# A second order table for a kernel whose instruction order is written out: fillers and transfers placed anew

## The chip, the cores and the metric

The kernel runs on one core of a Trainium2 chip. Five engines work side by side, each through its own instructions in the order in which they were issued: TensorE (PE in the profile, its weight loads PEld), VectorE (DVE), ScalarE (ACT), GpSimd (POOL) and SyncE (SP). SP does no arithmetic here: it issues every transfer between the device's memory and the on-chip buffers. The metric is the device time of one launch in microseconds (us), the median of three runs.

## The reference

The input `x` and the logits `f_logit` are 4 batches of 6272 time steps with 256 channels. First a gated recurrence runs along time, then a block that multiplies two projections with a third one that was convolved (circularly, over all 6272 steps) with a long filter:

```
f = lower_bound + (1 - lower_bound) * sigmoid(f_logit);   i = 1 - f
h[t] = f[t] * h[t-1] + i[t] * x[t]            # for every batch and channel
x1, x2, x3 = split(h @ w_proj, 3)             # 256 -> 3 x 256
conv = irfft(rfft(x2, time) * rfft(filter, time), time)
out = (x1 * conv * x3) @ w_out                # 256 -> 256
```

## The kernel before

The time axis of 6272 steps is taken as 128 x 49, so the transform is done in two steps of matrix products: one over the 128 (D1), one over the 49 with its twiddle factors (FT), and back (VA and VB, then ID). Four batches follow one another, and the work on the recurrence of batch b+1 is laid over the end of batch b.

The program is not written in the order in which it runs. `Plan.op` records operations: a kind, the engines that may do it, what it reads and writes, its function. `Plan.emit` then issues them in the order that a long string, `ORDER`, holds: three characters per operation give its number, its engine and its bank of PSUM (`Plan.order`). `emit` asserts that all that an operation depends on was issued before it. Each engine then runs its own operations in that order and waits by semaphores for the others. So the string decides three things: each engine's sequence (SP's too, hence the order of the transfers), who does a copy that two engines may do, and the PSUM banks. There are 2325 operations.

In what follows an operation is named by its kind and its number among its kind: `ff3` is the fourth load of filter rows. The kinds, with the lines of the kernel before:

- `warm` (L561): 32 fillers of TensorE, four products of a constant each, whose results nobody reads.
- `ff` (L579, SP): 13 loads of filter rows, 512 KB each (the last 128 KB), into ten buffers, so `ff10` to `ff12` wait for a buffer. `fr` (a copy, L270, L275 or L280): to one of two staging buffers. `rot` (L590, PE): a rotation of the rows, `f2` (two copies each, ACT or DVE): its result out of PSUM.
- `FF1`, `afs`, `FF2`, `hw`, `hst` (L615, copies, L633, L272 or L277, L641): the transform of the filter in 16 units; `FF1` needs all `f2`. `hst` (two per unit, 196 KB and 128 KB) stores the spectrum into the device's memory. `last` (L650) is the zero frequency's part.
- `args`, `tabs`, `rest`, `pad` (DVE, POOL): tables of sines and zeroed edges, made once.
- `load` (L308, SP): 13 chunks of 512 time steps per batch, two loads a chunk, an even number for `f_logit` (tile FL) and an odd one for `x` (tile XT), 512 KB each, the last chunk's 128 KB; three buffers, so the loads of chunk c wait for the transposes of chunk c-3. Chunk c of batch b has `load` 26b+2c and 26b+2c+1.
- `sig` (L311, ACT), `u` (L313, POOL), `su` (L325, PE), `f` (L338 ACT or L340 DVE), `scan` (L346, DVE): sigmoid, product with x, transposes to channels on the partitions, gate, recurrence. `su`, `f` and `scan` come twice per chunk. `wrap` copies the first 3072 steps of a batch behind its end.
- `P` (L673) and `x2`: the projection of x2, 13 groups, which need all scans of the batch. `F1` (L686), `A`, `F2` (L745), `prod` (L758, DVE), `I2` (L768), `Th`: 16 units of forward step, product with the spectrum, first inverse step. `H` (L723, SP) loads a unit's spectrum, 392 KB, into one of three buffers (tile Hu), which in the front are the staging of `hw` and `hst`.
- `x13` (L373), `xs`, `z` (L389, POOL): the other two projections and their product.
- `I1` (L802), `y` (L808, DVE), `proj` (L820), `o`, `store` (L830, SP): second inverse step, gate, output projection, and 13 stores of 512 KB a batch out of three buffers; they need all `Th` of the batch.

The numbers behind `ORDER` come from a planner that is not part of the kernel; the `cost`, `dma` and `lag` values that stand in the calls of `op` are not used at run time and are the same in both kernels.

Of the kernel before, what the change touches and what calls it, by code (L numbers as in the profile page):

```python
# [58 lines left out]
class Plan:  # L59
# [55 lines left out]


ORDER = (
    "A8gAAYBBgAOYABIAjQBLgACIBGgAtRBQgBVgAhSBagBkgAdTA7YAPIAxUBfgA9AA2VBpgAwWBCAA0XBugBDQA+SBFABMYBzgAyUBEAARIAvV"
    "BHYBACAqWA/CBNUA1XAQAB4gAmQERgBIRBWYAkWAcTBRAADgAYYAuXAnQBJBAgWBKBESgBSWAzTBUGBbYBXQBTGEpgAeSBYIBgYASABcSBPE"
    "BlIEdgAaYBZABhWBqABOMBmQEegBeKBdCBvYBrUBjOBnAEqgAUIBoAB0YAGgBwSBiOA4QATIBxCB5YB1WByKAFgAlRBsMB2GB6SAiQB7CBtM"  # L120
    "B8CA5RETAB3OAfQAWICISCBUCJKCKQEUYB/WCLACRSCCECAOA3QEfACNUAEYCOMCDYEVWErAEZQEgYEWGCEUE1gEaAE2gEXOCFEEbIEsYEhW"
    "ElUEiGCTQFBgCSCEjOFCgANACaSCQgAVYEmECMYCUIEtWCbCEnMAIACVYCWQAXYE3AExSEuOApUFNgAHAEyKArVE4YFOgCXACcUCHgEzKCGg"
    "AJAA6QFDAClQEvOE5SALACdEFEYCmIE9WE6CCjUE+OFZgAKAFagAsQE7KCkECYgCsQAMACeYFFUFPAEcYE/OCfSFGEFQYCgCFJWFHMFjgFKG"
    "CoSFkgCtACuUFLOCPgEwYCpCFRQE0YCvMFbAFVWCnYFSIC3SFtgFcYFWOFugAoUC4CCigC1UFTICZgCxSC2EFXOC6UCyCFAYFdQCwYFlAFMY"
    "FgSC7MC+WC5YF3gE8AFmYFhKF4gDAUC/GChgFeIDBECqgDJWCzgFfIAbUFvADCYFnUDKGFiKDDQFwYFoEFqWDEAFpMDHSGBgCrgDQQDICC0g"
    "FrODSUGCgFIYDRADbSFsOF5ADLYDMQDTMFxWDcCF6YDNIDVUFyGF0SDWEFzODZQGLgF1CC8gDiUFUYC9gDaADkWF2KGMgDUYDjEDdYDtQDGg"
    "B9YGDADFgDeUDlOF7SDuADfMDnWF8CDmYF+QDoGF9KD2UGEYGVgF/ADXgDrWDOgD3ED0SDsOD/UGWgD1CGAIDwWB+YDPgFYAGNADvYGFSD4Y"
    "EAMEoYD9QDxGGGKDggD5UGOYDhgGHKD+AGIWDYgD6EEGQMVgGJOEISDzgEHAGKOEBYGPUGXAEYAGSQEJCGQMECWGTAMhgEKYGYYGRMEPSDqg"
    "EDGDpgAZYEQCGUIGZWELUGaGEkYGcSJSQGbOGdCMtgEMEGeKJTRDygGfgEEgGmWJVJJUAENgMXAD8gJWYG4SGnOGgUEFgEOgG2QG5KD7gG0W"
    "G3AGhMGsSMjAGyQGtKG1GGqUMvAGiWGrMGkSGjGHLgGoUGlKHEgMigGwWGpEMWgHSgGuSGxGJXUGvKGzAJYVJcWJaFJdXJZMG8QJfHJeOJbY"  # L130
    "G6SG9AG+UG7KJhXJgYG/EHAQJiWHBAHFSJkOJmUJjHHHKJnVJoEJlYHCQHMWJpFHIKJrUJqYJsSJtEHDIJwVHZgJuCHiTHOOHGYJxQJvYHjD"
    "J1RJyNJ2SJzAHJTHPOJ3BJ0YHgVJ4CHTQHKDHqgHNYJ6XHUYHVIHhFJ5YHkSJ7UHlCHWIHQVJ/QJ9EHbYHRNHaSHxgJ8HKARKBAJ+YHcKHmU"
    "KCBHrWHnEMkYHdKHXQKESHYAHtOH4gHeUKGCIGQHuOKDYHfEHoSKFWIHAHyUHpKH/gKJXKHGH0MMugHsYIIQKLHKIYHvSIJAH1MH5WHzYHwC"
    "H6YIKQMYYH7OIQgKKUILAH2SH8OIAVH3CIMQICNKMEIXgH9SINAKNYKOXIDNKPUH+CKTVIBYKQHIOQIegIRSIPIKVFIsWKREITKIEQItGKSY"
    "KUVIUKKYUKWFKZSISYKaEKXYIYWIlgIFAKdVIaOKbCKeTIZYIVQKfFKcYIbOKgDIfUIWAKiSIhMI2gIuWIcQIvGIiMImTInYKkCKhYI3WIpL"
    "IdAI9gKjVKnSIgYKlFIwQIoLKpCKmYIjUIxAKoSJEgI5OKsTMwYKqCIqQIkEI6OKtSIrAMZUKvKKuDI+WJLgKrYMaEMdQJAOIySMeAM5gKwY"
    "M6gIzCMbMKxWKzGMlSMfIKyUMmCK2VJBOK0EK3WK4FMpQK1YK5GMnKI0UNFgMqAMxWK6YNGgI1MM7AM1SMrIK7UMgYNRgMyGK8VI4YNSgI/Y"
    "K9EM8YMzOI7QM2CLAUK+FM3KJFWI8ALBVLCEK/YJHOM9QLDFNBSNHALEYJIOLFUNdgM+ALGVNegLHENIYM/IJCWNCCLKUNTANDKJMQJDGJGY"
    "JOINJSNUYLIFNNWNKCJPINngNOGNogNfANLKLJYNVQLMELLVNPOLPUNWANgYNZSLRELNFNXILQUNxgNaCJJWNygLSERSVNbKLOYJKGNhQNpA"
    "NkWJNYNiILTYRTUN7gNlGRUNJQSN8gNqYRVENjIRXVJRCRYUNmORZFLZQRaELUSNzAMsYLaINrUNuWNsEN0YLVKOFgLbQNvGOGgNtMLWSLcA"  # L140
    "McYNwON9ALeULjQLXCN+YLfMN1WM0AN4SLYgLkIN2GLdgLoUOPgN5CN3OOQgLgQOHANAAN6KOIYLlWLhALpMLtSLigLmGN/QLuKNQYOCUOAA"
    "LqWOagMoAOBIOZgODELngLySLrGOEMOJQORAOMWLsgLzKLvUUVgONGOSYOKAOOOL0SLwEOLIL3WM4YObAOTULxgNMAL4ONEYOWQOUENYYUhg"
    "L1COcYOVML8WUigOXAOdSL2gL9OL5UOeCNcAOfKL+WL6EOYIOgSUXAMBUOhKMGQOiKL/GOrSMHIMAgOvWOsCMCMUugOnQUWgOwGUtgO5SL7g"
    "OoAOzUO6KOlWO0EOjQOmOOxSOkAOpUUjAO1WOqMOyCMDQO2GO7SMEIOtUO8CMLWOuEMQQO3SMMOUvAMIUO4CUwYMNWMRIMJMO9QMOGO/SO+I"
    "PBUPACRWYPDWPCMPHQPEGRbYPNSPJIPFWRcURdVReEPGORhQRfFPKIPgWRjARgYRiUPhGRmVPQKPZgPiQPIYRkEPLWPjAPPKPTTPUYRlYRoF"
    "PaQPVLPqgPMGRnSRrVPOYRpCPWLPRWRtFPmSPSGPbYPcIRqYPkUPxgPnCPXWPdIRsQPlEPrSPYGRwRP4gPtKPoURuAPeWRyBPpMRvYRxQPuK"
    "PyRRzAPsYQGUPfGPzYUYYP1JP/gR1QQHEPvWP0JP5SR3AQIUPwGP7KR0YQQgP2QQJEQAWP8KP6YP3AQKUQBYR2SQLEQCOP9QQXgR4CR6TQDO"
    "QRUP+AR5YR7WR8DQTMQMQQegR9GUkYR/SMPgQNAQEWQUMQYTSBCQFGQOQSASQaLQlgR+YSEVMKgSCCSFWQPIUZSSDYSGFQbLQuQSHGSJXQvA"
    "QSYUaKQsVSIYQ2gSKUSLPQtFQVQUbKQZYSOXSMEQfVQWASNYSPUQhNSQHQwSSREQcQQxCQiNQmUQnYSSYQdAQySQpMQ9gUdWQzCQgYSTQQoM"
    "UeGSURQjSSVAUfOREgSWBQqUU5gQkCSXYU6gQ0QQ3WQ1IUgAMFgQ+SQrEQ5OQ/YSYQSZRSaASdURAKSbBSeVSfEUlQScYQ6OSgFSiWUmASjS"  # L150
    "Q4YSkGRBKShYRLgSnUSlCSoVU7AQ7WUnISmYRFSSqFSpMQ8GU8YUpQRHKSsVUqAVFgStUVGgSuFRCWRIKSvESxSSrYRDGSyVUrIRMTSwYUxW"
    "S0FRPLU1QSzCUyGS2VRGYVRgS1YROLS3SVSgS4FS7US5CS8VRNYUzOVHARJSS6YU2AS+NRQWVIYRKCU3ITAVRRGU9SS9ETBQU+KTCFVBWS/Y"
    "TDIVTAVJUVdgU/KTFRVegTEYVCGTGQTHBVDOVNSTIAVUYTKRVKEVngTLQTMBVogVLMMSWVOCTNATPRVPKTJYVVUTQQVWEMTOTOYVZSTRJTSA"
    "TUWVfAVXMVygTTYZSQMUgZTRVaCVxgVQYTVOZXUZUAVgYZYVZVBZZMZaFTWWVpAVbKTZQTXGU4YVhUTaIVqYVkSViETYgTeWV7gVlCVjMTbQ"
    "V8gUcAVmKTcAVrUVsETfOTjQTdgVzAVuSTkITgWWFgVMAV0YVvCVtMTlQU0AThGVwKToUV9ATigV1WWGgTpMV4SV2GV+YWPgV5CV3OTqUWQg"
    "TmAV6KTtWTngTrEUsYTyQVcYTuOWHAV/STsgWCUVAATzITvWWagWDEWZgWACWEMT3QWIYTwGWBKT8UUoATxgT0WWRAT4IVEYWJSWSYT9MWMQ"
    "WKCWNAWLKT5UT1GVYYWOIUBST2gT6EWTWUCKWWQWUGT7gT+UWbAcVgWVOWXAWcYUDST/EWYIWdWUAgWgUWeGchgWhEULQWfOUECctgWiMUGW"
    "cWgW3UUHOcugcigWvSUFgW4EUMIW5WWwKWzUW6GWlQW0EWjSWmAWtWWkKcXAW7UWrQcjAW8MWpSWsAWxUcYYWuGW1QWyMcvAWnWW2AUIUWoO"
    "WqCckYUNQUJMW9SUOAUQWW+KXBUW/QUROXAAXDSXCMZWYXHWXECXNQXKOZcUZbYXFSZdVZeEXGKZhXZfFXJOXgSZjHZgYXiUXhCZiXXQIXZg"
    "ZmWXIYZkHcZSXOYZoGXPIZlYcaCcdWXjEZnRcbKc6gZrQXqgceGZsUc5gZtIclSZpBcfOZuEXRQZqYcmCXaUXSAcnKXbYXmWXLQXnGXcMcpS"  # L160
    "XUYXMAZvYXTWXdMdFgZwUcqCZxQZyEXWOZ1RZzAXkUZ3BZ0YZ2QXVOXlEZ6XZ7RcwYcrKZ8HXeUXxgZ4AX4gXXWXfEdGgZ9JXoSc7AXYOXyU"
    "Z5YYIQXpKXrWYJAYGSc8YXtOcxQYHCXuOZ/WcyAaASaBGZ+YaETX1MX/gaCCaFXdHAXzYX0Mc1VXsYaDYaGDaJSdSgaHHczIXvTdRgc2FaIY"
    "YQgaKXXwDc3NX2QdIYaLCX5TX3AaOSX8LaMHaPVaQCYKQaRFX7LYAWaNYYLAYMUYDOaTSYXgYBYYNEaUTaSYaYQYCOaVCaZRaWDX6Yc9UaaA"
    "aXYYOSYegadXc+EYPKUKgaeWabBc/MYESdTAX9QagOafHYRUYSYX+AacYaiWYUMYFCYsQYZYajXYtAahYYTMYYSanVakGYaKc0YYlgYVQalH"
    "apFYuWamYYbKYWAYfUaoSYvGcgYYiMY2gYwQYgYaqCdUYYcWYxAYhMYmSasVYdGYoKY9gYyQauFYnYYjWarYYzAYpKY3UYkGY0QatSY1IZEg"
    "ccAaxTY5MYqWazDavCdBQY6MYrGawYY+TaySdCAZALa2WZLga0CY/Ya3XY4Yddga4Ga1Ya7VUPgdDIa5HY7SdegZMWcsYa9FZBLZFQa6YY8C"
    "a8VZHIZCSa+FbAUa/YZDCZPObBVbFQbCEdJSZGYbDFZIIbHAdNUbEYdKCbGXZOOdogZJQdngZNYbIHc4YdLKUSWZKAbJYdfAbKQdOMbLRdVS"
    "UTGdPMdgYbMAdZWbNBbPQdWCdxgdaObQRbRAdygZQUdXKbSBUUgbOYhSQZREhTRdbOdhSbTYhVBbZUhUAdMYdkWdpAbaMbUQd7gdlGdqYd8g"
    "bVIhXUdiChYVdzAdjKbWQhZEdAYdmOhaFbeSd0YbXAdrUbfKduWdsEbYgbbQeFgdvGdtMeGgd1SbcAdwObjUd9Ad4QbdgbkMbgWePgd2Cd+Y"
    "eQgd5Ad3KblUbhGd6IboSbmEbigdEYd/WeHAcoYbpKbngbtUeCQeIYbuMbqSeDAeZgeageAGeEIbvUbrCeBObyQbsgeRAeJSbzIeMWeKCeSY"  # L170
    "eNGeLKb0QeOObwEb8SdYYdQAeTUbxgb9Kb3Wb1Ab4OeWSeUEb2gcBQeXCeVMb5WebAecYeYKb+Ub6GcCIb/EcGSb7gedWeeOegUcDQefOehE"
    "dcAeiMcHKexWezUeyGcISe0McEAerWcJKe7QesGelUcKgepSe8AcAgetWeqKemEe5QeuGe3Ue6AcQScLWe4EcRKevQcMOe1SewIhWYenUe2C"
    "hbYejWeoMhcQekGhdRheIhhShfBe9ThjKhiVhgYe+De/WfBQfAOhkFfDSfCAhlYfHUhmWfECfKMhnXfNQhpHfJMfFShrVhoGhsXhqYhtFfGK"
    "hwWfZghuHfgUfQIhxShvYhyGh1TfhEfPIfiWfIYh2RhzCfLUfjOfqgh4Bh0Yh6Qh3DfTRfMEfOYh7TfWJh5Yh8AfRWh9DfkUfVJfSGh+YfaS"
    "flEh/QfcKfxgfUYfmWfbYiARfnGiBIiEUiFVfdKiCBfXWiGEiDYfrQfYGf4gfoSiJUfpKiHFgGWftIiIYiKVgHGfeSiLMiMFiOQfsYfzYfuI"
    "gIWffCiNYfyUiQAf5Sf1MgJGf/giPRiTQiRBf0MfvWiVAiSYiUVfwGf8Kf2QgQgf6YiWFgKWf3Af7KiXYgAUgLGgMQgDMgBYgXgf9SgNAiYW"
    "gCMiZXiaGgRQf+CgOVidUgeggPNibHcFggsSgTIgSYgEVicYgtCieXifMgFFiiQgUIguSigHgYUikAihYgfWglggbMgvCijRinQgZYilBgaM"
    "gVSipAgwQgWCggYghOimYg2ggcUgxAgmSgiOgnYgdEioWgyQiqGgpKg9ggjUgzAirYisXgkMitWiuHixTivGgoKg0Qg3UizDiwYg+Wg1IiyT"
    "hEgg6Mi2Sg4Yi0DgqQi4Ci1Yi3Tg5MgrAi7Vi8Si9FhBOhLgg7Qi5DjAUi+Ci6YhAOjBVg8AhFSg/YhMQjCEhHKi/YhCWjDFjFUhIKjEYhDG"
    "jGVjKSjHEcNWhOIhGYjIFjJYjLThPIhJUjNDjMCjPQhNYhKEjQTjOYjRIhQRjSLcSUhRBjTYcOGjUQjZScTEjVIcPgjeWcUgjjUjaKjWQjbS"  # L180
    "jXAjfOjcCjYgjkMjgQjdgjoWjhAjtSjpOjlUjigjqQjmEjuKjyWjngj3UjrAjzOjvSjsgj0QjwCj4Mj8Wjxgj5Sj9Oj1AkBUj2gkGQj6CkCM"
    "j+Wj7gkDSj/GkHIkLUkAgkIWkECkMMkFgkQQkNSkJOkRIkKgkSUkOCkPgkTEkUg"
)


# [706 lines left out]
```

## Time and profile before

| | |
|---|---|
| median of three runs | 476.97 us (475.66, 476.97, 477.04) |
| profiled execution, first to last instruction (its span) | 476.4 us |
| HBM read, written | 80.93 MB, 31.00 MB; 235 GB/s over the span |
| granted TensorE clock, mean | 0.998 |

The profile is of one execution, and its span is its own time; the median of the three runs is 0.6 us longer. `A <- B` in a group names what is written and what is read; "idle before" is the time in which an engine waited, with what ended the wait. The milestones of the profiled execution, read from the timeline:

| batch | first scan | last scan ends | first P | last P ends | first I1 | last store issued |
|---|---|---|---|---|---|---|
| 0 | 29.6 | 78.8 | 78.7 | 89.7 | 153.6 | 253.5 |
| 1 | 130.7 | 178.3 | 178.3 | 191.0 | 252.5 | 355.4 |
| 2 | 222.3 | 282.5 | 282.7 | 293.6 | 357.0 | 451.4 |
| 3 | 303.8 | 386.5 | 386.6 | 399.3 | 449.6 | 472.7 |

The stretch up to 78.7 us, in which the filter is transformed and batch 0's recurrence runs, is called the front.

### The profile page before, as it was taken

What the parts mean: (1) busy time and instruction counts of PE and PEld (TensorE: products, weight loads), DVE (VectorE), ACT (ScalarE), POOL (GpSimd) and SP (SyncE); (2) the same over time, 40 slices, a digit from 0 to 9 for tenths busy, and PEclk for the clock granted to TensorE, in tenths of its full rate; (3) what the DMA queues carried; (4) which work ended last, traced back from release to release, by engine and by line L of the source; (5) the groups of instructions that cost most, each with busy time, mean ns of one, the idle gap of its engine ahead of it and who ended that gap; (6) DMA issues with size and microseconds to landing.
All of it is one profiled execution on the core that took longest, in us unless ns stands there. A gap on an engine that the chain in (4) does not pass through costs nothing.

```text
span 476.4 us, 14713 instructions
## 1 busy us (share of the span) xinstructions
PE 447.8 (94%) x6041; PEld 345.4 (72%) x6041; DVE 424.9 (89%) x457; ACT 416.1 (87%) x606; POOL 297.9 (63%) x309
## 2 busy tenths in 40 slices
PE   8888999999998999999999999999999799999995
PEld 7776777866756879776666889666767697676784
DVE  8778989799999996999999996999999877999874
ACT  5899898899999998889999978999999778999763
POOL 6777784287889730668798734688787504766600
PEclk9999999999999999999999999999999999999999
DMA  8989998636588897157769995567588831356277
GB/s 329 396 310 317 313 342 251 227 104 216 165 289 306 289 328 279 41 164 226 244 230 312 345 338 219 145 205 235 163 271 270 341 135 46 110 152 193 77 279 277
DMA packets 39841, 112.88 MB, mean 237 GB/s; under 512 B 4258, under 2 KB 6178, under 8 KB 39774
## 3 DMA queue, kind: packets, MB, share of 16 engines
q1 hardware_dynamic: 39774, 111.94, 69.0%
q8 instruction: 47, 0.77, 0.6%
q14 instruction: 20, 0.16, 0.1%
HBM read 80.93 MB, written 31.00 MB: 235 GB/s over the span
## 4 chain that ended last, share of the span: by engine, by line
PE 52%; DVE 16%; DMA 12%; POOL 6%; ACT 6%; issue 6%; SPq 0%; ACTq 0%; DVEq 0%; POOLq 0%
PE PS L373 13%; PE PS L673 9%; DVE HA L346 8%; PE PS L768 8%; PE PS L745 6%; PE PS L686 5%; DVE ys L808 5%; PE PS L325 4%; DMA XT<-in_x_dram 4%; DMA X<-in_moe_filter_fft_dram 4%; PE PS L820 3%; POOL zt L389 3%; POOL XT L313 3%; DMA out_dram<-osb 2%; DVE PP L758 2%
## 5 line engine op out<-in xcount | busy, mean ns | idle before, releaser
L389 POOL TENSOR_TENSOR zt<-x1s,x3s 128x490 f16<-128x490 f32 (+1 forms) x104 | 125.5, 1214 | 67.1 <-ACT x3s L270 33.0
L313 POOL TENSOR_TENSOR XT<-XT,FL 128x1024 f32<-128x1024 f32 (+1 forms) x52 | 116.9, 2248 | 64.7 <-ACT FL L311 41.8
L758 DVE TENSOR_TENSOR PP<-PS,Hu 98x1008 f16<-98x1008 f32 x128 | 146.5, 1198 | 4.9 <-PE PS L745 2.7
L346 DVE TENSOR_TENSOR_SCAN HA<-fTs,HA,PS 128x512 f16<-128x512 f32 (+1 forms) x96 | 112.5, 1201 | 5.1 <-ACT fTs L338 4.3
L373 PE MATMUL PS<-HA,W 128*128 128x490 f16 (+1 forms) x416 | 104.5, 368 | 1.3 <-ACT Th L270 0.6
L808 DVE TENSOR_TENSOR ys<-PS,zt 128x1024 fp32r<-128x1024 f32 (+1 forms) x52 | 58.8, 1150 | 8.5 <-PE PS L802 6.5
L820 PE MATMUL PS<-Wo,ys 128*128 128x256 f32 x392 | 57.8, 293 | 3.5 <-DVE ys L808 2.5
L270 ACT CAST HA<-PS 128x1024 f16<-128x1024 f32 x57 | 57.2, 1025 | 3.7 <-PE PS L686 3.6
L338 ACT ACTIVATE fTs<-PS,nomc 128x512 f32<-128x512 f32 (+1 forms) x86 | 56.2, 672 | 4.8 <-PE PS L325 4.3
L272 ACT ACTIVATE osb<-PS 128x1024 f32<-128x1024 f32 (+1 forms) x46 | 45.0, 985 | 16.9 <-DMA out_dram<-osb 8.7
L768 PEld LDWEIGHTS <-PP 98*128 98x128 f16 x1024 | 49.7, 98 | 11.7 <-POOL PP L750 2.1
L270 ACT COPY x3s<-PS 128x490 f32<-128x490 f32 (+1 forms) x96 | 54.6, 574 | 4.0 <-PE PS L373 1.8
L820 PEld LDWEIGHTS PS<-Wo,ys 128*128 128x128 f32 x392 | 49.3, 188 | 9.0 <-DVE ys L808 4.6
L272 ACT ACTIVATE x1s<-PS 128x490 f32<-128x490 f32 (+1 forms) x89 | 52.1, 592 | 3.9 <-PE PS L373 2.2
L373 PEld LDWEIGHTS <-W 128*128 128x128 f16 x416 | 33.4, 97 | 30.4 <-issue 8.3
L311 ACT ACTIVATE FL<-FL 128x1024 f32<-128x1024 f32 (+1 forms) x52 | 52.8, 1019 | 2.1 <-DMA FL<-in_f_logit_dram 2.0
L325 PE MATMUL PS<-iden,FL 64*128 64x64 f32 x784 | 45.8, 232 | 8.6 <-DVE HA L346 2.2
L325 PEld LDWEIGHTS PS<-iden,FL 64*128 64x128 f32 x784 | 33.7, 138 | 27.0 <-DVE HA L346 9.0
L768 PE MATMUL PS<-VA,PP 98*128 98x98 f16 x512 | 51.8, 207 | 0.6 <-POOL PP L750 0.2
L270 ACT CAST Th<-PS 128x784 f16<-128x784 f32 x61 | 50.2, 830 | 1.8 <-PE PS L768 1.2
L768 PE MATMUL PS<-VB,PP 98*128 98x98 f16 x512 | 51.6, 207 | 0.0
L673 PE MATMUL PS<-W,HA 128*128 128x256 f16 x392 | 44.6, 274 | 0.2 <-DVE HA L346 0.2
(110 smaller groups left out, 685.7 us busy)
## 6 DMA issues: line engine op xcount, KB each, us to landing
FL<-in_f_logit_dram SPq DMA_DIRECT2D x48, 512.0 KB
XT<-in_x_dram SPq DMA_DIRECT2D x48, 512.0 KB
out_dram<-osb SPq DMA_DIRECT2D x48, 512.0 KB
Hu<-H SPq DMA_DIRECT2D x55, 392.0 KB
X<-in_moe_filter_fft_dram SPq DMA_DIRECT2D x9, 512.0 KB
H<-Hu SPq DMA_DIRECT2D x16, 196.0 KB
H<-Hu SPq DMA_DIRECT2D x16, 128.0 KB
Hu<-in_moe_filter_fft_dram SPq DMA_DIRECT2D x2, 512.0 KB
```

What stands on the lines that cost most here:

```text
L270: nc.scalar.copy(dst, src)
L272: nc.scalar.activation(dst, src, AF.Copy, scale=scale)
L313: op("u", {"POOL": 0.1 + 0.553 * nb}, lambda e, xt=xt, ft=ft: nc.gpsimd.tensor_tensor(xt, xt, ft, op=AOP.mult), r=[("ft", k)], w=[("xt", k)])
L325: nc.tensor.transpose(bank(pb)[:, at[p] + j:at[p] + hn:nb], src[ps, j, cols], iden[ps, ps])
L346: nc.vector.tensor_tensor_scan(h, fT, bank(pb)[:, 512 - hn:512 + hn], init, op0=AOP.mult, op1=AOP.add),
L373: nc.tensor.matmul(PS[:, p, 0:n], W13[:, kh, js], HA[:, HB[kh] + t0:HB[kh] + t0 + n], start=(kh == 0), stop=(kh == 1))
L389: nc.gpsimd.tensor_tensor(late["zt"][:, jb, :, m0:m0 + nm], xs(0), xs(1), op=AOP.mult),
L673: nc.tensor.matmul(pp[:, r - r0, :], column(HB[kh], q_of(r)), W2[:, kh, :], start=(kh == 0), stop=(kh == 1))
L758: nc.vector.tensor_tensor(PP[:TB, k, o, :, :, 1:64], px.unsqueeze(1).broadcast_to([TB, 2, UE, 63]), hh[:, :, :, 1:64], op=AOP.mult)
L768: nc.tensor.matmul(PS[:, ib + o, pr * TB:(pr + 1) * TB], PP[:TB, k, o, n, 2 * pr:2 * pr + 2, :], v[:TB], start=(n == 0), stop=(n == 1))
L808: nc.vector.tensor_tensor(late["ys"][:, yk, :, 0:rn * 128], PS[:, cb:cb + 2, 0:rn * 128], late["zt"][:].rearrange("p k r m -> p k (r m)") ...
L820: nc.tensor.matmul(po[:, i, :], late["ys"][:, yk, kh, i * 128:(i + 1) * 128], Wo[:, kh, :], start=(kh == 0), stop=(kh == 1))
```

## The change

The string `ORDER` is replaced; nothing else in the kernel differs. The diff is therefore 65 lines of characters out and 63 in (the new string has the same 2325 operations):

```
 ORDER = (
-    "A8gAAYBBgAOYABIAjQBLgACIBGgAtRBQgBVgAhSBagBkgAdTA7YAPIAxUBfgA9AA2VBpgAwWBCAA0XBugBDQA+SBFABMYBzgAyUBEAARIAvV"
...
+    "EegAAYAjQAwQAOYA5QABIACIAsQAeQAgQAvQA7YA2QBBgBCAAdQAfQA8gA9YBLgAuQAyQAPIBGgBVgBQgAlQAtQAcQBDQBMYA+SBHYA/KAQAATIB"
...
 )
```

Decoded, the places that matter read as follows (each line one engine's sequence; `...` where operations are left out).

```
SP, start
- ff0 ff1 ff3 ff2 ff4 ff5 ff6 ff8 ff7 ff9 ff10 ff11 ff12 load0 wcol0 load1 load4 load2 load3 load5 wl1 wl0 load6 load7 load8 load9 hst3 load10 load11 hst1 hst0 load12 load13 ...
+ load3 ff1 ff0 ff3 ff2 ff5 ff4 ff6 ff7 ff8 ff9 ff10 ff11 ff12 wcol0 load0 load1 load2 load4 wl0 load5 load6 hst1 load7 load8 load9 load10 load11 hst4 hst7 hst0 load12 load13 ...
SP, end of the front
- ... load24 hst18 hst16 load25 hst17 hst20 hst21 hst19 load26 hst25 load28 hst23 hst22 load30 hst24 hst28 hst30 hst27 hst29 hst31 hst26 H1 H0 load29 load27 H2 H3 ...
+ ... load25 load24 hst14 hst19 wl1 hst22 hst21 hst17 hst18 hst16 load29 load28 load31 load30 load27 load26 hst27 hst23 hst25 hst29 hst28 hst31 hst24 hst26 hst30 H0 hst20 H1 H2 H3 ...
SP, second and fourth recurrence
- ... load48 load49 store2 load51 load50 store3 store4 load52 ...    ... load98 load99 store27 load100 load101 store28 ...
+ ... load48 load49 store2 store3 load50 store4 load51 store5 ...    ... load98 load99 load101 load100 store27 store28 ...
PE, start
- warm x8, rot1 rot0, warm x3, rot3, warm x2, rot2, warm x5, rot4, warm, rot5, warm, rot6 rot7 rot8 rot9 rot10 warm rot11 warm rot12 warm x3, FF12 FF11 FF13 FF10 FF14 warm FF21 su0 su1 ...
+ warm x15, rot1 rot0, warm, rot3 rot2 rot5 rot4, warm x3, rot6 rot7 rot8, warm x2, rot9 rot10 rot11 rot12 FF10 FF12 FF13 FF11 FF21 FF16 FF20 su0 su1 ...
PE, end of the front
- ... su22 su23 FF214 last0 su24 FF215 su25 x130 x131 P3 P12 P0 ...
+ ... su24 FF215 su25 x130 x131 last0 FF214 P6 P0 P11 P8 x132 P4 x133 ... P12 x134 x135 x136 x137 F12 F10 F11 x138 x139 F20 ...
DVE, start
- turns args0 args2 f210 fr8 f26 f213 f215 tabs1 f214 tabs0 f221 f218 f219 f223 tabs3 afs2 afs0 hw1 scan0 scan1 scan2 ...
+ turns args0 f20 tabs0 tabs1 args2 f213 f29 fr10 f217 fr11 fr12 f221 f222 f225 afs0 tabs3 afs3 afs1 hw1 hw0 scan0 scan1 scan2 ...
```

`wl0` and `wl1` are the loads of the two weight matrices (768 KB and 256 KB), `wcol0` that of the lower bound. Of the 32 fillers, all stood in the front; now 22 do, and ten stand later: three among `x13` and `I2` of batch 0's last units, one among batch 1's last `x13`, one at the start of batch 1's `I1`, one in batch 2's first units, two in batch 2's `I1` stage and two in the last `I1` stage. POOL's two zeroing operations `pad1` and `pad2` stand ahead of `u0`; before, they stood behind `u9` and `u10`. A few copies change hands between ACT, DVE and POOL (for example 17 `x2` go from ACT to DVE and 10 the other way; 11 `wrap` from ACT to POOL and 3 the other way).

## The prediction

> **What bounds the kernel now.** First the page: span, engines, and the busy tenths of the forty slices.
>
> ```profile
> span 476.4 us, 14713 instructions
> PE 447.8 (94%) x6041; PEld 345.4 (72%) x6041; DVE 424.9 (89%) x457; ACT 416.1 (87%) x606; POOL 297.9 (63%) x309
> PE   8888999999998999999999999999999799999995
> DMA  8989998636588897157769995567588831356277
> ```
>
> No engine is free to take work: PE, DVE and ACT are all near nine tenths. So the question is what ends last in each stage. The busy times by stage (front, three batch periods, last batch; columns are length, then PE, PEld, DVE, ACT, POOL busy, the granted clock, the transfers' share and GB/s):
>
> ```profile
> 0.00:78.00 78.00, 69.41 (x770) 54.81 (x771) 67.17 (x101) 67.06 (x99) 58.78 (x80) 1.00 0.92 324
> 78.00:180.00 102.00, 97.77 (x1394) 74.44 (x1393) 95.91 (x97) 94.25 (x140) 67.58 (x62) 1.00 0.74 246
> 180.00:290.00 110.00, 106.22 (x1494) 83.14 (x1492) 100.18 (x100) 100.15 (x145) 67.14 (x61) 1.00 0.73 244
> 290.00:390.00 100.00, 95.02 (x1366) 72.01 (x1365) 93.40 (x93) 89.11 (x133) 68.74 (x64) 1.00 0.65 216
> 390.00:477.00 87.00, 79.37 (x1026) 60.98 (x1024) 68.26 (x70) 65.54 (x92) 35.63 (x42) 0.99 0.46 161
> ```
>
> In the front the transfers are busiest (0.92); in the middle PE is busy 95 to 97% and DVE 91 to 94%, so little idle is left for any order to win there. The timelines of PE, DVE and SP give the front's milestones: fillers, first rotation, first FF1, first and last scans, and the issue that waits for the first freed buffer.
>
> ```profile
> 1.34 6.57 PE L561 MATMUL PS<-iden 128*128 128x256 f16 x32 [1.34 <-POOL iden masks.py:199]
> 7.67 1.19 PE L590 MATMUL PS<-afs,rot 128*128 128x256 f32 x8
> 24.26 2.59 PE L615 MATMUL PS<-D1r,f 128*128 128x256 f32 x20
> 29.65 2.33 DVE L346 TENSOR_TENSOR_SCAN HA<-fTs,PS 128x512 f16<-128x512 f32 x2 [0.36 <-ACT fTs L338]
> 77.72 1.08 DVE L346 TENSOR_TENSOR_SCAN HA<-fTs,HA,PS 128x128 f16<-128x128 f32 x2 [0.27 <-ACT fTs L338]
> 29.16 0.34 SPq L308 DMA_DIRECT2D FL<-in_f_logit_dram  x1
> ```
>
> The chain that ended last shows where transfers are on it: a load of x in the front, one of the logits in batch 2's I1 stage, and stores at the end.
>
> ```profile
> 40.28 8.28 DMA XT<-in_x_dram
> 366.38 8.92 DMA FL<-in_f_logit_dram
> 456.68 4.24 DMA out_dram<-osb
> 463.30 4.76 DMA out_dram<-osb
> ```
>
> **The change, part by part.** The sum is made against the profiled span of 476.4 us; the median of the runs, 476.97, lies 0.6 above it, which is added at the end.
>
> *The filter stage.* Fifteen fillers instead of eight stand ahead of rot1. In the PE timeline the first seven start 0.85 us apart, the later ones 0.44. So 7 x 0.85 + 8 x 0.44 = 9.5, and rot1 starts at 1.34 + 9.5 = 10.8 instead of 7.67. load3, now ahead of the filter rows, delays each of them by one transfer: SP's issues that wait for a landing (11.04, 12.33, 13.61, 14.89, 16.17 in its timeline) stand 1.28 apart. The rows' first copies would then be done at about 7, before the fillers; so load3 itself is covered by them (1.28 if they were gone). On DVE, f20 now stands ahead of args2 and waits for rot0 (12.0). Then come tabs (1.6) and args2, which ran from 8.09 to 14.14, 6.05: until 20.2. Behind args2 stand f213 and f29, which free PSUM banks of rot6 and rot4. rot8 needs the first (20.8), the two fillers and rot9 the second (21.4; rot9 at 22.3). fr11 follows rot9 (22.9), rot11 at 23.5, rot12 at 24.1, and the last copies f223 and f224 on ACT (0.6 each) end at 25.5. First FF1: 25.6 instead of 24.26, +1.3. Then sig0 (a table load of 1.28 and 1.07) ends at 27.9; u0 (2.37) at 30.2, with pad1 and pad2 (1.70 and 0.8) done ahead of it by 27.5, hidden by sig0. DVE now does hw1 and hw0 (1.22 each) before scan0; hw0 waits for FF20, which ends at 30.4, so scan0 starts at 31.7 instead of 29.65: **+2.1**. Bounds: 0 (if the three waits overlap better than my walk) and +3.5.
>
> *The scan stage of batch 0.* By the mean durations of the rows DVE does, from scan0 to the last scan, 26 scans 29.4, 7 afs 4.3, 11 f 7.4, 3 hw 3.6: 44.7 in 49.2 us. In the new order it does 26 scans, 6 afs 3.6, 13 f 8.0, 1 hw 1.2: 42.2. That is 2.5 saved if DVE sets the pace. The other pace-maker is the loop of three buffers: 8.28 transfer, sig 1.07, u 2.37, su about 0.8 make 12.5 per three chunks, 4.2 a chunk against DVE's 44.7 / 13 = 3.4; then nothing is saved by DVE. Both appear in the waits, so I take half, **-1.2**; bounds 0 and -2.5, and for the loop see the rival.
>
> *The end of the front.* last0 (0.56) and FF214 (0.70) move behind the last su and x130, x131, ahead of the first P. Before, they ran while PE waited for ACT. P needs the last scan anyway, about 0.9 behind su25, covered by the two x13; so 1.26 more lands on the path, less what su25 gains: **+1.0** (0 to 1.3).
>
> *Ten fillers later.* Ten times 0.44 on PE. The two in the last I1 stage cost nothing: that stage is paced by 13 stores (4.24 and 4.76 on the chain), and their order is unchanged; with faster stores they would cost 0.9. The other eight, 3.5, fall where PE is 95 to 97% busy; in the O stages DVE is busy 100% of 140 to 160 us and PE 18.0 of 20, so most are covered. I take a quarter, **+0.9**; bounds 0 and 3.5.
>
> *Transfers in the middle.* load100 and load101 go ahead of store27, one 512 KB store (1.6 at 324 GB/s) earlier, in the stall of 8.92: 0 to -1.6. load50 and load51 go behind store3 and store4: 0 to +2. Taken together **0**.
>
> *Batch 1's loads before the spectrum.* Six loads of batch 1 now stand ahead of the last nine hst and H0. Four of them (2.1 MB) leave when the last su frees the buffers, then 1.4 MB of hst, then H0, 0.4 MB: 3.9 MB at 324 GB/s is 12 us, with 2 us for the last landing 14. The first prod comes 13 P (10.9), 8 x13 (3.7), 3 F1 (1.3) and F2 (0.8) after the first P, 16.7. **0**, covered by the P stage; if the rate is 211 GB/s, as between 80 and 100 us, it is 18.5 + 2 and costs up to 4.
>
> *Copies that change hands.* x2 goes to DVE, which is idle for 3.4 of 80 to 100 us in the P stage; eight more wrap (0.62 each) go to POOL, busy 63%. 0; without the cover 0.6 per wrap that holds a u, 2 in all.
>
> Sum: 2.1 - 1.2 + 1.0 + 0.9 = +2.8: 479.2 by the span, **479.8** as a median.
>
> [...] In the row, fillers run at half pace for 5.9 us. [...]
>
> **The rivals.**
>
> *Faster: the transfers pace the front and the new queue feeds it better.* For it: the share of 0.92, the 8.28 of the chain, and POOL's 17.9 us of waits for x. Ahead of the last loads of batch 0 stand 15 hst instead of 18 and w_out (256 KB) moves behind them: 0.74 MB, 2.3 us. With DVE's 2.5, the whole late start is made up, and the store in the 366 us stall gives 1.6: 476.97 + 2.1 + 1.0 - 2.5 - 2.3 - 1.6 - 0.5 for six fillers (2.6 of PE, mostly idle time) that leave the scan stage, **473.2**. It decides when the scan stage takes under 46 us instead of 49.2. Against it: late in the front no row waits for a load (the last waits are for ACT and PSUM).
>
> *No change:* the three batch periods have the same work in nearly the same sequence (14, 11 and 12 scans stand ahead of the first y in both orders), and DVE's 2.5 cancel the late start: **477.0**.
>
> *Much slower: H0 late and the fillers at full price.* The rate of 211 GB/s holds while writes run; 479.8 + 2 (half of 4) + 1.7 is **483.5**. It decides when the first prod comes more than 17 us behind the first P.
>
> **How the numbers follow.** My walk (478.4 to 482): 0.36, much slower 0.13, no change 0.16, faster 0.35. A measurement of this kernel can tell about 0.3%, 1.4 us, from no change. Hence slower 0.49, same 0.16, faster 0.35. The time is my walk's, 479.8, own range 478.4 to 482. For eight in ten the range must take in both signs: from 471.5 (the faster rival with 1.6 more from a second and third recurrence stage) to 486 (much slower with its upper bounds).
>
> **What would show it.** First rot row near 10.8, first L615 row near 25.6, first scan near 31.7, first L673 row near 80.5; a PE row of L561 past 140 us beside no longer a batch period than 100 to 104 us; POOL and DVE not waiting for Hu at the first product. The prediction is wrong if the first scan is late and the first P is not, or if a batch period changes by more than 2 us, which would say that the small permutations in the middle outweigh the front.

## The result and the profile after

The changed order takes 479.15 us in the median of 20 runs, the one before 476.56 in 20 runs beside them. The ratio is 1.0051, 95% interval 1.0032 to 1.0070: slower by half a percent, 2.6 us, where +2.8 was forecast. The page of the changed kernel, the lines that answer to those of before, with its row of TensorE's granted clock:

```profile
span 477.1 us, 14701 instructions
PE 448.9 (94%) x6041; PEld 347.9 (73%) x6041; DVE 423.9 (89%) x457; ACT 412.0 (86%) x599; POOL 302.1 (63%) x316
PE   8779889999999999999999889999999999999996
PEclk9899999999999999999999999999999999999999
DMA  8958998835587888255687987376679751444167
```

No engine's total has moved by more than 4.2 us. What is new is the second slice of the clock row: TensorE's granted clock is 0.50 from 15.3 to 18.7 us, which is called the half clock below, and 1.00 around it. Before, that row read:

```profile
PEclk9999999999999999999999999999999999999999
```

The busy times by stage, in the same columns as before:

```profile
0.00:78.00 78.00, 66.08 (x713) 51.09 (x713) 66.25 (x99) 63.72 (x95) 58.41 (x77) 0.98 0.87 310
78.00:180.00 102.00, 98.43 (x1409) 75.68 (x1406) 95.31 (x98) 93.67 (x137) 70.36 (x68) 1.00 0.72 248
180.00:290.00 110.00, 104.82 (x1483) 82.05 (x1482) 100.30 (x99) 96.19 (x141) 68.62 (x64) 1.00 0.70 238
290.00:390.00 100.00, 98.41 (x1423) 76.81 (x1422) 95.25 (x94) 91.17 (x136) 69.05 (x65) 1.00 0.70 243
390.00:477.00 87.00, 81.12 (x1026) 62.25 (x1024) 66.76 (x70) 67.31 (x93) 35.70 (x42) 0.99 0.41 149
```

PE, DVE and ACT all did less in the first 78 us (713 products against 770), so the front is late. Its milestones, from the timelines of PE and DVE of the changed kernel:

```profile
1.34 8.50 PE L559 MATMUL PS<-iden 128*128 128x256 f16 x60 [1.34 <-POOL iden masks.py:199]
9.60 1.18 PE L588 MATMUL PS<-afs,rot 128*128 128x256 f32 x8
15.91 2.78 PE L559 MATMUL PS<-iden 128*128 128x256 f16 x12
26.88 2.32 PE L613 MATMUL PS<-D1r,f 128*128 128x256 f32 x16 [1.68 <-ACT f L268]
33.20 1.22 DVE L344 TENSOR_TENSOR_SCAN HA<-fTs,PS 128x512 f16<-128x512 f32 x1 [0.20 <-ACT fTs L336]
79.45 0.48 DVE L344 TENSOR_TENSOR_SCAN HA<-fTs,HA,PS 128x128 f16<-128x128 f32 x1
79.39 0.56 PE L648 MATMUL PS<-mX,FTr 64*98 64x128 f32 x8
79.79 0.66 PE L631 MATMUL PS<-afs,FTr 64*98 64x512 f32 x4
80.38 3.85 PE L671 MATMUL PS<-W,HA 128*128 128x256 f16 x32
```

Line numbers are two less than before. Two rows of before, to compare the third row and the last one with:

```profile
8.70 1.48 PE L561 MATMUL PS<-iden 128*128 128x256 f16 x12
78.65 11.02 PE L673 MATMUL PS<-W,HA 128*128 128x256 f16 x98
```

The first rotation is 1.9 us later than before, the first FF1 2.6, the first scan 3.5, the first P 1.7 (80.38 against 78.65). The third row stands in the half clock: 12 products of three fillers take 2.78, where 12 took 1.48 before. From the first P to the end of the span it is 396.7 us, before 397.8. So in these two profiles the change loses 3.5 us in the filter stage, wins 1.8 in the scan stage and the end of the front together, and about 1 behind it.

What lies around a span was mis-set in the prediction, which took 0.6 us for it. Each execution is on record with its time and its span: the changed kernel's 20 have 2.47 us around the span in the mean, 65 of the kernel before, timed beside the other runs, 1.96. What makes this half microsecond is not shown. So the profiled execution of before, with a span of 476.4, took about 478.4 us, an estimate from these numbers; that is above the highest of its 20 times (478.05). The changed kernel's profiled execution, 479.51, lies near its median. Hence the spans differ by only 0.6 us and the medians by 2.6, and the "about 1 behind it" may be nothing but this one long execution: in a second profile of the kernel before (below) the stretch from the first P to the end takes 396.6 us.

### The profile page after: what moved, and what is told of

Read it like the earlier page. It is cut to its first block, busy times and chain, and to the rows that moved or that the text cites. A ratio compares the mean times of both kernels' runs of the same rounds, so it can differ in the third digit from the quotient of the medians.

```text
span 477.1 us, 14701 instructions
## 1 busy us (share of the span) xinstructions
PE 448.9 (94%) x6041; PEld 347.9 (73%) x6041; DVE 423.9 (89%) x457; ACT 412.0 (86%) x599; POOL 302.1 (63%) x316
## 4 chain that ended last, share of the span: by engine, by line
PE 65%; ACT 12%; DMA 10%; DVE 6%; issue 5%; POOL 2%; SPq 0%; ACTq 0%; DVEq 0%; POOLq 0%
PE PS L371 16%; PE PS L766 8%; PE PS L671 7%; PE PS L323 6%; PE PS L743 6%; PE PS L684 6%; PE PS L818 6%; DMA FL<-in_f_logit_dram 6%; DMA out_dram<-osb 4%; PE PS L800 3%; PE PS L559 3%; ACT osb L270 3%; DVE HA L344 2%; ACT fTs L336 2%; ACT Th L268 1%
## 5 line engine op out<-in xcount | busy, mean ns | idle before, releaser
L371 PE MATMUL PS<-HA,W 128*128 128x490 f16 (+1 forms) x416 | 102.0, 368 | 2.9 <-ACT osb L270 1.1
L268 ACT CAST HA<-PS 128x1024 f16<-128x1024 f32 x61 | 61.3, 1029 | 3.2 <-PE PS L684 3.0
L270 ACT ACTIVATE osb<-PS 128x1024 f32<-128x1024 f32 (+1 forms) x49 | 47.9, 990 | 14.9 <-PE PS L818 8.3
L371 PEld LDWEIGHTS <-W 128*128 128x128 f16 x416 | 34.8, 97 | 33.9 <-issue 9.0
L818 PE MATMUL PS<-Wo,ys 128*128 128x256 f32 x392 | 56.8, 291 | 2.5 <-ACT osb L270 1.5
L270 ACT ACTIVATE x1s<-PS 128x490 f32<-128x490 f32 (+1 forms) x91 | 53.6, 597 | 3.3 <-PE PS L371 1.6
L268 ACT CAST Th<-PS 128x784 f16<-128x784 f32 x63 | 52.3, 839 | 1.0 <-PE PS L766 0.5
```

Source lines behind the costliest of these rows:

```text
L268: nc.scalar.copy(dst, src)
L270: nc.scalar.activation(dst, src, AF.Copy, scale=scale)
L371: nc.tensor.matmul(PS[:, p, 0:n], W13[:, kh, js], HA[:, HB[kh] + t0:HB[kh] + t0 + n], start=(kh == 0), stop=(kh == 1))
L818: nc.tensor.matmul(po[:, i, :], late["ys"][:, yk, kh, i * 128:(i + 1) * 128], Wo[:, kh, :], start=(kh == 0), stop=(kh == 1))
```

## The experiments

All are orders made from the two tables: an operation moved, or a stage of one order joined to the rest of the other, with the operations' dependences and the PSUM banks kept. Where the number of fillers changes, `WARM` changes with it; their results are read by nobody. Each was timed against the kernel before on the same chip, 6 to 12 executions each. The three rounds ran on three chips, where the kernel before took 476.38, 477.17 and 477.10 us, so runs of different rounds are to be compared by their ratios. The milestones are of one profiled execution each. The theories at the start: A, the prediction's, that the filter stage's late end makes the loss; B, that the ten late fillers make it on a busy TensorE; C, that the many small permutations of the batch periods make it. D, formed after the first round, is A with the half clock: D1 holds the clock for the cause, D2 for a symptom.

| run | median us | ratio to before, 95% interval | first FF1 | first scan | last scan ends | first P |
|---|---|---|---|---|---|---|
| before (first profile) | 476.56 | | 24.3 | 29.6 | 78.8 | 78.7 |
| changed | 479.15 | 1.0051, 1.0032 to 1.0070 | 26.9 | 33.2 | 79.9 | 80.4 |
| without late fillers | 480.05 | 1.0067, 1.0043 to 1.0090 | 26.9 | 33.2 | 79.5 | 80.0 |
| args2 first | 484.37 | 1.0156, 1.0118 to 1.0194 | 30.1 | 37.1 | 83.6 | 84.0 |
| old front, new rest | 480.15 | 1.0071, 1.0048 to 1.0095 | 24.6 | 30.0 | 78.4 | 80.4 |
| new front, old rest | 487.37 | 1.0220, 1.0192 to 1.0248 | 27.1 | 33.4 | 81.2 | 83.5 |
| before, again | 477.94 | 1.0017, 0.9991 to 1.0043 | 23.9 | 30.1 | 78.8 | 78.6 |
| old filter stage | 473.82 | 0.9928, 0.9898 to 0.9958 | 23.5 | 29.5 | 77.6 | 78.1 |
| five fillers more | 477.31 | 0.9992, 0.9971 to 1.0013 | 25.9 | 32.9 | 78.5 | 79.0 |
| new filter stage in before | 481.36 | 1.0086, 1.0059 to 1.0114 | 26.8 | 32.9 | 80.7 | 80.5 |
| load3 back | 479.84 | 1.0061, 1.0037 to 1.0086 | 26.4 | 33.3 | 82.1 | 82.7 |
| eight fillers first | 477.00 | 0.9994, 0.9967 to 1.0021 | 23.9 | 30.2 | 77.9 | 78.4 |
| eight first and five more | 478.22 | 1.0033, 1.0015 to 1.0051 | 24.5 | 31.7 | 78.3 | 78.7 |
| old filter stage, no late fillers | 475.13 | 0.9959, 0.9940 to 0.9977 | 23.8 | 29.9 | 76.7 | 77.1 |

**First round: the late fillers, one move, and two joins.**

```
changed order, PE:  - the ten `warm` behind su25
```

> The changed order without its ten late fillers (22 are left, all in the front). Theory A (the filter stage's late start makes the loss, the late fillers cost a quarter of their 4.4 us): 1 us less than the changed kernel, about 478.2. Theory B (the ten fillers on a busy TensorE make the loss): back to the kernel before, 476.6, or below. Theory C (the small permutations of the three batch periods make the loss): no difference from the changed kernel, 479.2.

480.05, not faster than with them; the intervals overlap. Theory B falls, and with it the quarter of their time that theory A charged: ten fillers of 0.44 us on an engine that is busy 95% of the time cost nothing that shows here. "No difference" is what theory C had expected; the second round tests it.

```
changed order, DVE:
- turns args0 f20 tabs0 tabs1 args2 f213 ...
+ turns args0 args2 f20 tabs0 tabs1 f213 ...
```

> The changed order with one operation moved: DVE does args2 right behind args0, ahead of f20, as before the change. Theory A: args2 then ends near 14 us instead of 18.4, the banks of rot6 and rot4 come free earlier, the first FF1 row stands 1 to 1.5 us before 26.9 and the first P about as much before 80.4; time about 478. Theories B and C: front a little earlier, time within 0.5 us of the changed kernel's 479.2.

484.37, and the first FF1 at 30.1: 3.2 us later, not earlier. All three theories missed this. The new place of args2, behind f20, which the prediction held to be harmful, is a good one for the rest of this order. PE's waits of this run between 7 and 32 us (in total, times, longest):

```profile
PE PS L588 <- ACT f L268: 5.5, 3, 4.2
PE PS L613 <- ACT f L268: 1.7, 1, 1.7
```

A rotation waited 4.2 us for a copy of ACT, and DVE's f20 ran at 14.58, behind args2, instead of 10.90. The other copy of the same rotation stands next on ACT; with the banks not freed, rot2 and all behind it waited. In the same profile the clock is half from 14.5 to 21.3 us, so not all of the loss need be the wait's own.

```
front: before, all operations of batch 0 ahead of its first P, and the first loads of H
rest:  changed order, late fillers out          (and the reverse)
```

> The front in the order before (all 32 fillers in it), everything from the first P of batch 0 on in the changed order, without late fillers. Theory A: the first P near 78.7 as before, the batch periods neutral, time 476.6 within 0.7. Theory B: the same, 476.6. Theory C: the periods keep their loss, 478 to 479.

> The front in the changed order (its 22 fillers), everything from the first P on in the order before, no late fillers. Theory A: the first P near 80.4, 1.7 later than before, and all of it is passed on: 478.3. Theories B and C: the late start is taken up by the waits of the middle: 476.6 to 477.

480.15 and 487.37. Read alone they would say that the middle is what is slow, theory C. But the joints spoil both. In the first, P starts 2.0 us behind its last scan, and the first product waits behind an x1s that waited 2.95 for POOL; in the second, the P stage takes 17 us instead of 11, with one wait of 3.39 for a copy on ACT. Neither wait appears at that size in the profiles of before or of the changed kernel, so both runs say little about the stages; the next round joins at the first FF1 instead, where both orders have done the same operations.

**Second round: the filter stage alone.**

```
kernel before, unchanged
```

> The kernel before, unchanged, for a second profile of it and for what lies around its span. All theories: time 476.4, TensorE's clock whole through the front, first FF1 near 24.3, first P near 78.7. If its time is about 2.4 us above its own span, as in the runs of the changed orders (479.5 with a span of 477.1), the first profile of before (476.4) was of a slow execution, and a usual span of it is near 474.

477.94, the same within noise, and 2.0 us around the span instead of 2.4. The first profile was of a long execution all the same, as worked out above; by the median of 476.56 a usual span is near 474.6. The clock of this one was not whole: half from 31.8 to 35.2. So even the order before loses the clock in some executions.

```
iden iota turns args tabs0 tabs1 rest0 rest2 pad0 ff fr rot f2 load0..5 and the fillers among them:
  order before, 25 fillers;   all other operations: changed order
```

> The changed order with the filter stage alone as before: filter rows, their copies, rotations, tables, first six loads, and the 25 fillers that stood among them (36 in all). Everything from the first FF1 on is in the changed order. Theory D (the loss is the filter stage's late end and the half clock in it, the rest is neutral or better): clock whole from 7 us on, first FF1 near 24.3, first scan 30 to 31, first P near 77.5, time 475.5 to 477. Theory C (the loss sits in the middle): first P near 77.5, time still 478 or more.

473.82, 0.72% faster than the kernel before and, by the ratios, 1.2% faster than the changed one; theory D had expected less of it. C falls: with the filter stage put back, the rest of the changed order is faster than the old rest. This kernel beats both. Its profile is not free of the half clock either: half from 50.3 to 53.7 us, in the scan stage.

```
the same set in the changed order, 21 fillers;   all other operations: order before, 7 fillers
```

> The order before with the filter stage alone as in the changed kernel (21 fillers there, seven later in the front as before, none after it). Theory D: half clock at 15 to 19 us, first FF1 near 26.9, the rest of the front as long as before, first P near 81, time 2 to 3 us over before: 478.5 to 479.5. Theory C: the late start is taken up, 476.5 to 477.

481.36, 0.86% slower than before, about 4 us: more than expected and in the same direction. The filter stage alone makes a loss, in either company: 0.86% with the old rest, 1.2% with the new one, 4 to 6 us.

```
changed order, PE:
- rot1 rot0 warm rot3 rot2 rot5 rot4 warm x3 rot6 ...
+ rot1 rot0 warm x2 rot3 warm x2 rot2 warm rot5 warm rot4 warm x3 rot6 ...
```

> The changed order with five more fillers between rot0 and rot4, where TensorE idles before its clock falls to half at 15.3 us; nothing else moves. Theory D1 (the half clock makes the filter stage late): no half clock between 10 and 20 us, first FF1 at 25.2 to 26, time 1 to 1.5 us below the changed kernel, about 478. Theory D2 (the order of copies and banks makes it late, the clock is a symptom): clock whole, first FF1 still 26.7 to 27.3, time 479 to 480.

477.31, the same as before; the ratio is 0.6%, 2.8 us, below the changed kernel's, and the intervals do not overlap. In the stretch from 15 to 19 us the changed kernel and this run read (third from the end is the granted clock):

```profile
15.00:19.00 4.00, 3.92 (x20) 3.19 (x21) 3.23 (x10) 3.56 (x6) 0.95 (x1) 0.57 1.03 408
```

```profile
15.00:19.00 4.00, 3.21 (x27) 2.69 (x26) 3.79 (x11) 3.80 (x7) 1.83 (x3) 1.00 1.02 404
```

With more work on TensorE the kernel is faster: in this profile the clock is whole there, 27 products instead of 20 go through, and the first FF1 comes 1 us earlier, as D1 expected. The half clock was not gone, however; it fell later, from 26.2 to 29.7 us. The mean clock of every execution is on record: 0.993 to 0.996 in these twelve, 0.987 to 0.996 in the changed kernel's 20, of which five are below 0.993.

**Third round: what of the filter stage.**

```
changed order, SP:
- load3 ff1 ff0 ff3 ...  load1 load2 load4
+ ff1 ff0 ff3 ...  load1 load2 load3 load4
```

> The changed order with load3 at its old place, behind load2, so that the filter rows go first again; nothing else moves. Theory D (the transfer is covered by the fifteen fillers and by args2): first FF1 within 0.5 us of 26.9, time within 0.7 of the changed kernel, 478.5 to 479.8. Rival (the transfer delays every row and the stage with it): first FF1 near 25.6, time near 477.8.

479.84, no difference. The half megabyte ahead of the filter rows is covered, as the prediction had it. Its profile shows something else besides. TensorE's sequence is that of the changed kernel, but the clock happened to be whole from 6.8 to 27.2 us:

```profile
10.44 1.19 PE L588 MATMUL PS<-afs,rot 128*128 128x256 f32 x8
26.39 3.11 PE L613 MATMUL PS<-D1r,f 128*128 128x256 f32 x16 [1.26 <-ACT f L268]
```

So without the half clock among the rotations the first FF1 still stands 2.1 us later than before. The clock of this profile fell at 27.2 and again at 54.5, and its scan stage took 48.8 us and not 46.7.

```
changed order, PE:
- warm x15 rot1 rot0 ...
+ warm x8 rot1 rot0 ...
```

> The changed order with eight instead of fifteen fillers ahead of rot1 (25 in all); nothing else moves. By the prediction's walk: rot1 near 7 us, first FF1 about 1.3 earlier, 25.6, time near 477.8. By theory D1: the seven fillers also kept the clock up; without them the half clock comes as early or longer, first FF1 no earlier than 26.5, time 479 or more.

477.00, by the ratio 0.6% (2.7 us) below the changed kernel; the first rotation at 6.71, the first FF1 at 23.90, 3.0 earlier. The walk had the direction and about the time, but less than half of the gain at FF1. In this profile the clock stays whole with seven fillers fewer, but the profile is not typical: its mean clock of 0.999 is the highest of the twelve, the other eleven have 0.983 to 0.996, and the mean of all, 0.9925, is no higher than the changed kernel's 0.9934. So the clock was no better, as D1 said, and the kernel gained nevertheless, against D1: what the seven fillers cost is their length and not the clock. The twelve times spread from 474.25 to 481.40, the widest of all.

```
changed order, PE: both edits, warm x8 first, five fillers between rot0 and rot4
```

> Eight fillers ahead of rot1 and the five more of the clock run between rot0 and rot4. If the late rot1 is the rest of the loss: first FF1 near 24.5, time 475.5 to 476.5. If args2 behind f20 and the banks are the rest: first FF1 near 25.9 as with fifteen, time 477 to 477.6.

478.22, a ratio of 1.0033: the two gains do not add, the first FF1 at 24.5 as the first case said, the time near neither. In its profile the clock is half from 24.1 to 27.5, where FF1 begins.

```
old filter stage as above, without the ten late fillers
```

> The run with the old filter stage (473.8) without the ten late fillers, 26 left. If the late fillers cost a quarter of their 4.4 us: 472.7. If they cost nothing, as without them in the changed kernel: 473.3 to 474.4.

475.13, 0.41% under before, no faster than with the late fillers, and above both of the times expected. For the second time they cost nothing. The intervals of the two runs with the old filter stage overlap, so the new rest is worth 0.4 to 0.7%, 2.0 to 3.4 us.

## Why the prediction was right, step by step

The forecast, the sign and the place hold: the loss is made in the filter stage, the scan stage gives part of it back. The size of +2.8 is right within 0.2, and that is luck. By the runs that exchange the stage, the new filter stage costs 4 to 6 us, where the sum had 2.1 and at most 3.5; all the rest of the new order, which in the sum loses 0.7 (-1.2 + 1.0 + 0.9), wins 2.0 to 3.4. The two errors cancel. The single terms below are read from one profile of each kernel.

*Filter stage, +1.3 to the first FF1 and +2.1 to the first scan: right in place, too small.* It measured +2.6 and +3.5, at the upper bound of 3.5. Its parts: The fifteen fillers: with eight, the first FF1 is 3.0 us earlier and the time 2.7 less, so this is the largest part, as predicted in kind. They took 8.26 us (1.34 to 9.60), not 9.5. The 5.9 us of slow fillers behind that price were those of one execution. In it the fillers start 0.85 us apart until the clock is first whole, at 7.32 us, and 0.44 apart from then on; in the changed kernel's profile the spacings are the same, but the clock is first whole at 5.03. In the second profile of before rot1 began at 6.74 instead of 7.67. The place of args2: wrong. The walk let f20 wait and args2 run late, which happened (args2 ended at 18.4), but took it for a cost; args2 ahead of f20 costs 5 us more. The half clock between 15.3 and 18.7: not in the sum at all. The prediction looked at the slow fillers of the first microseconds only, and not at whether the clock would fall again in the new gaps between the rotations. The end of the stage: up to rot9 the walk's times came true (rot8 at 20.8, measured 20.81; rot9 at 22.3, measured 22.18), with rot1 1.2 and args2 1.8 us earlier than it had them and the half clock in between. What the walk lacked came behind it: rot11 waited 0.49 for a copy of DVE, and ACT did three of the last copies in a row until 26.83, where the walk let two end at 25.5.

*Scan stage of batch 0, -1.2 (0 to -2.5): inside its bounds.* It took 46.7 us instead of 49.2 (first scan to the end of the last), 2.4 of the 2.5 that DVE saves by the sum of its rows. That would fit DVE as the pace-maker, not the loop of three buffers. But with the new filter stage and the old rest, where DVE does its old work, the stage took 47.8 us: 1.4 of the 2.4 came without the new order of the scan stage. So which of the two sets the pace is not shown, and half was a fair guess.

*End of the front, +1.0: +0.6.* The first P stands 0.45 behind the last scan's end where it stood 0.15 ahead; last0 and FF214 in the last rows above are what is between.

*Late fillers, +0.9: nothing,* twice (ratio 1.0067 without against 1.0051 with; 0.9959 against 0.9928). The lower bound was the value.

*Loads of batch 1 ahead of H0, 0: right.* H0 left at 89.9 instead of 85.9, but the first product followed its F2 by 0.65 us, before by 0.76. (It came 17.1 us behind the first P, just over the 17 by which the rival was to be known, but DVE waited there 0.19 for TensorE and not for a load.) *load3, covered: right.*

*Middle, 0: open.* From the first P to the end, three profiles with the old rest take 397.8, 396.6 and 398.3, nine with the new one 395.2 to 398.6, 396.6 in the mean (the two runs with spoiled joints left out). The means differ by 1 us, but the spread is 3.4. The total hides shifts. From one first P to the next, the third period is shorter in the changed kernel, by more than the 2 us that the prediction had named as a sign that it was wrong:

```profile
282.70:386.60 103.90, 98.92 (x1404) 75.95 (x1401) 96.23 (x95) 92.79 (x137) 68.74 (x64) 1.00 0.69 232
286.70:387.50 100.80, 99.25 (x1430) 77.61 (x1429) 96.05 (x95) 91.89 (x137) 69.05 (x65) 1.00 0.70 240
```

The first line is before, the second the changed kernel. In the second profile of before this period took 102.1, so part of the 3 is the long execution's; over the same twelve profiles the new rest makes the first period 1.2 longer, the second 0.3 longer, the third 1.7 shorter and the last 0.7 shorter, in the means. The runs that exchange the filter stage still put the loss there and not in the middle. By the two runs with the old filter stage, scan stage, end of the front and middle together win 2.0 to 3.4 us; how much of it is the middle's was not told apart.

*The rivals.* "Much slower" did not come: its two causes, H0 and the fillers, cost nothing. "Faster" was to be known by a scan stage under 46 us; it took 46.7. The stage did get shorter, whether through DVE or through the transfers is not shown, and the kernel is faster as soon as the filter stage is left alone.

How does the lateness of the filter stage divide between the late rotations and the half clock? At the first FF1 the profiles tell: with fifteen fillers and half clock among the rotations (four profiles, the run with args2 first left out) it stands at 26.8 to 27.1, with fifteen and whole clock there at 26.4 and 25.9, with eight and whole clock at 23.9 and 24.5. So by these profiles the half clock is worth some 0.5 to 1.0 us there and the seven fillers 1.4 to 2.5. For the time it stays open: by the ratios each edit takes back 2.7 or 2.8 us, both together 0.9, and in each of these profiles but the one with eight fillers the half clock came back later.

## What to carry to other kernels

When an order is searched with a cost model, test its stages separately: here one stage of the new table lost 4 to 6 us and hid a gain of 2 to 3.4 in the rest, and the joined order beats both. Join two orders only at a point where both have done the same operations; the joins elsewhere made waits of 2.95 and 3.39 us of their own. Here five more fillers in the gaps between the first products took 2.8 us off the time, and seven fewer ahead of them 2.7 us; both edits together took off 0.9, so such a choice has to be timed. And one profile is one execution: place it among the times of the others before its stretches are compared.

## What the runs showed of the hardware

In these profiles TensorE's granted clock fell to 0.50 after stretches in which its products were busy for 22 to 62% of the time. In the changed kernel's profile the clock is first whole at 5.03 us, falls at 15.27 and is whole again from 18.68, which is 10.24 and 13.65 us behind the first; in the first profile of before it is whole from 7.32 to 474.9. In all 14 profiles each change, the ends of the programs left out, stood at a multiple of 3.41 us from the first (spans at full clock of 10.2, 17.1, 20.5, 27.3, 34.1 us, at half of 3.4 or 6.8); what sets this step is not shown. I divided each of the 14 profiles into such stretches, counted the busy time of PE's products in each, and looked at what came next. Leaving out the ends of the programs, the clock fell fifteen times, and the stretch just before was busy for 22 to 62%. No stretch busy for more than 62% was followed by a fall; all five below 46% were; between 46 and 62% ten were and sixteen were not, so the busy time alone does not decide there. Three of these stretches, of the changed kernel, of the run with args2 first, and of the one with eight fillers (length, then PE busy):

```profile
11.90:15.30 3.40, 2.11 (x14) 1.52 (x13) 3.26 (x14) 3.40 (x7) 3.00 (x5) 1.00 1.02 407
```

```profile
11.10:14.50 3.40, 0.74 (x4) 0.54 (x4) 3.19 (x10) 0.00 (x0) 1.89 (x4) 1.00 1.02 408
```

```profile
8.70:12.10 3.40, 2.36 (x16) 1.61 (x14) 2.94 (x14) 2.76 (x4) 3.01 (x4) 1.00 1.02 418
```

After the first, 62% busy, the clock was half for 3.4 us; after the second, 22%, for 6.8; after the third, 69%, it stayed whole. The clock was first whole at 4.3 to 7.3 us, another time in each of these profiles, so stretches counted from there lie over other operations each time.

Of the executions without a profile the mean clock is on record, and it goes with the time. Of the changed kernel's 20, the five with a mean clock of 0.996 took 476.4 to 477.8 us, the five with 0.992 or less 479.3 to 482.0; over all 20 the correlation is -0.82. With eight fillers the four below 0.993 took 478.3 to 481.4, seven of the other eight 474.3 to 477.4; but the eighth, with 0.999, took 479.45, so the clock is not all. The kernel before had 0.993 to 0.999 in 65 executions, with a weaker correlation (+0.2, -0.3 and -0.5 in the three rounds). That an order with more half clock spreads more fits this; which order meets it how often was not worked out.
